# Two sequences per scan, VectorE in GpSimd's place, blocks of 512 tokens, and weight tiles in pairs: one kernel of attention and two MoE layers

## The chip, the core and the metric

One of the eight cores of a Trainium2 chip runs the kernel: TensorE (matmuls, PE in the profile, with PEld for its weight loads), VectorE (DVE), ScalarE (ACT), GpSimd (POOL) and SyncE (SP, which issues the DMA transfers here). The metric is the device time of one execution in microseconds. Three runs of the kernel before took 1298.25, 1298.7 and 1300.54 us, a median of 1298.7.

## What is computed

The reference, cut to what matters. Four sequences of 768 tokens, 8 heads of width 48, go through a recurrence with a complex decay; its output, 3072 tokens of 384 values, goes through two dense layers with different activations (`moe` and `moe2`; nothing is routed).

```python
# q, k, v, a_re, a_im: (4, 8, 768, 48)
mag = np.sqrt(a_re * a_re + a_im * a_im)
scale = np.minimum(mag, 0.999) / (mag + 1e-06)
a_re_n, a_im_n = (a_re * scale, a_im * scale)
for t in range(S):
    ar, ai = (a_re_n[:, :, t, :, None], a_im_n[:, :, t, :, None])
    new_re = ar * S_re - ai * S_im
    new_im = ar * S_im + ai * S_re
    kv = np.einsum('bhd,bhe->bhde', k[:, :, t], v[:, :, t])
    S_re, S_im = (new_re + kv, new_im)
    y[:, :, t] = np.einsum('bhd,bhde->bhe', q[:, :, t], S_re)
x = y.transpose(0, 2, 1, 3).reshape(3072, 384)
h = x @ w_in                                   # w_in (384, 2048)
x = (h * (1.0 / (1.0 + np.exp(-1.702 * h)))) @ w_out   # w_out (2048, 384)
h = x @ w2_in
out = (h - np.tanh(h)) @ w2_out
```

The weights come as float64 (random numbers of numpy) and are handed to the device as pairs of 32-bit words.

## The kernel before

**Attention.** A sequence is cut into 6 chunks of 128 tokens (`C`), so there are 24 sequence chunks (`NU`), worked on in the order of chunk number first and sequence second. A chunk passes four generators. `s1` (L342) scales the decay and runs the first level of a prefix product: 16 runs (`NS`) of 8 tokens (`L`) lie on the partitions with the heads, and the loop over `j` (L371) multiplies complex numbers along a run. `s2` (L381) carries the products across the 16 runs in four doubling steps, each of which shifts data between partitions by a DMA (L391). `s3` (L403) multiplies both together (L410 to L414), divides k by the product and multiplies q with it (L438, L441). `s4` (L445) transposes both on TensorE (L465), makes scores (L479), masks them (L481), forms y from the state (L488) and from the chunk (L492), and updates the state of the sequence (L502 to L513). `transposed` (L518) then splits the chunk's 384 values per token into a rounded part `xh` and a rest `xl` for matmuls.

GpSimd shares the elementwise work: `PT` is its two-input operation (L349 to L368, L410, L438, L513, and in the MoE layers L203 and L248), `TT` and `STT` are those of VectorE, `ACT` those of ScalarE. The first three chunks (`BORROW`) use buffers of the weights.

**The MoE layers.** A block is 384 tokens (`TB`, three chunks, `BU`), so there are 8 blocks for each of the two layers. `moe` (L527) runs, for each block and each of the 16 tiles `f` of 128 hidden values, `h_tile` (9 matmuls into bank `h`: three chunks of the contraction, each as rounded times rounded, rounded times rest, rest times rounded, L138 to L140), a gate (`gate1` or `gate2_small`, which also splits its result into `gh` and `gl`), and `out1` or `out2` (9 matmuls into the banks `o`, and in the second layer `y`), three steps later (`LAG`). Each matmul streams 384 columns. Two sets of `xh` and `xl` exist (L143). The first layer's output goes to DRAM (`store1`) and comes back for the second (`load_o`).

**Weights.** `wsplit` (L97) turns one tile of 128 x 384 float64 weights into a rounded part and a rest: two operations on ScalarE, four on VectorE (L111 to L114), a rounding copy on ScalarE (L116), a product, a difference and a sum on GpSimd (L117, L119, L121; the very first tile's difference on VectorE, as are those of the second layer). There are 32 tiles in each layer.

**Order.** Every generator is given a start and an end (`add`, L601), by tables and rates (`SLOT`, `DC`, `BL`, L606 to L672); the steps of all are sorted by due time and emitted (L675), and a scheduler then orders each engine's queue. An engine runs its queue in that order.

PSUM has eight banks: `h` 2, `at` 2, `o` 3, `y` 1 (L91). A second path (from L682) recomputes everything if a range check failed; it is not taken with these inputs.

Of the kernel before, what the change touches and what calls it, by code (L numbers as in the profile page):

```python
# [41 lines left out]
def attention_moe_moe(ctx, tc, q, k, v, a_re, a_im, w1_in, w1_out, w2_in, w2_out, out):  # L42
# [11 lines left out]
    TB = 3 * C  # L54
# [30 lines left out]

    h4 = cp.tile([P, NBLK * NF], F32, name="h4")

    GL = 5
    BORROW, WA = 3, 8
    SQ = 1  # L90
    BANKS = {"h": 2, "at": 2, "o": 3, "y": 1}  # L91

    def psum(pool, tag, bufs):
        return pool.tile([P, 512], F32, tag=tag, name=tag, bufs=bufs)


    def wsplit(pools, wpool, tag, bufs, src, name, rawpool=None, sub=None):  # L97
        cm = pools["cm"]
        rp, rtag, rbufs = rawpool or (cm, "raw", 2)
        raw = rp.tile([P, 2 * DM], I32, tag=rtag, name=rtag, bufs=rbufs)  # L100
        dma(out=raw.rearrange("p (c x) -> p c x", c=src.shape[1]), in_=src)
        yield
        w3 = raw.rearrange("p (n w) -> p n w", w=2)
        lo32, hi32 = w3[:, :, 0], w3[:, :, 1]
        w = wpool.tile([P, 2, DM], F32R, tag=tag, name=tag, bufs=bufs)
        v_ = cm.tile([P, DM], F32, tag="cv", name="cv", bufs=3)
        vi, l_ = v_.bitcast(I32), lo32.bitcast(F32)
        ACT(out=v_, in_=hi32.bitcast(F32), func=AF.Abs, scale=65536.0)
# [18 lines left out]
    def w_in_src(src, f):  # L127
# [680 lines left out]
```

## Time and profile before

| | us |
|---|---|
| median of three runs | 1298.7 |
| the profiled execution | 1300.61 |
| its span, first to last instruction | 1298.9 |
| first matmul of the first MoE layer, block 0 | 175.2 |
| block 1 | 298.4 |
| block 7, the last of the first layer | 814.8 |
| first block of the second layer | 877.0 |
| its second block | 934.8 |
| last matmul | 1286.2 |

The starts of blocks are those of each block's first h matmul (288 matmuls make a block). Durations of VectorE and ScalarE reach from start to written result, and neighbours overlap a little, so that the distance of two starts is what an operation takes in a full queue. GpSimd's spans are rough. TensorE's ends are modelled; distances of starts are exact.

### The profile page before, as it was taken

How to read it: one execution, taken by the hardware profiler on the slowest of the kernel's cores; microseconds unless marked ns; L12 is line 12 of the kernel's file. 1: busy time of each engine (PE TensorE's matmuls, PEld its weight loads, DVE VectorE, ACT ScalarE, POOL GpSimd, SP SyncE). 2: the span in 40 equal slices, each digit the busy share in tenths (PEclk: the TensorE clock that was granted, in tenths of full speed). 3: DMA queues.
4: the chain of work that ended last, by engine and by line, in shares of the span. 5: the costliest groups of instructions: out<-in, count | busy, mean ns of one | idle time of the engine just before them, and what ended most of it. 6: DMA issues, size and time to landing. Idle time of an engine off the chain costs nothing.

```text
span 1298.9 us, 19212 instructions
## 1 busy us (share of the span) xinstructions
PE 1086.9 (84%) x6496; PEld 1057.8 (81%) x6496; DVE 891.3 (69%) x2089; ACT 735.5 (57%) x1553; POOL 582.1 (45%) x482
## 2 busy tenths in 40 slices
PE   0004678789979999999999999978999999999996
PEld 0004668778979988999988998878999999999996
DVE  6998999989988778878687729898333333333332
ACT  4323454555645464454464536667767777777673
POOL 5676767664533333333333205667434434434331
PEclk9999578788889899989998998999999999999998
DMA  5112322333213112232231104441001001000000
GB/s 170 58 49 84 94 73 75 102 88 85 61 45 81 51 51 67 54 83 54 57 81 41 46 21 144 139 122 37 28 10 37 19 19 38 13 25 25 1 19 24
DMA packets 114052, 77.01 MB, mean 59 GB/s; under 512 B 69904, under 2 KB 109840, under 8 KB 113936
## 3 DMA queue, kind: packets, MB, share of 16 engines
q1 hardware_dynamic: 113936, 75.61, 20.8%
q8 instruction: 55, 0.90, 0.3%
q14 instruction: 61, 0.50, 0.1%
HBM read 53.48 MB, written 9.44 MB: 48 GB/s over the span
## 4 chain that ended last, share of the span: by engine, by line
PE 42%; DVE 30%; ACT 7%; DMA 6%; POOL 6%; issue 6%; SPq 0%; DVEq 0%; POOLq 0%; ACTq 0%
PE o L139 5%; PE o L140 5%; PE o L138 5%; PE h L138 4%; PE h L140 4%; PE h L139 4%; DVE a L376 3%; DMA shifted<-x 3%; PE at L138 3%; PE at L140 3%; PE at L139 3%; DVE cv L113 2%; DVE gl L167 2%; DVE pq L373 2%; DVE cv L111 2%
## 5 line engine op out<-in xcount | busy, mean ns | idle before, releaser
L197 DVE SCALAR_TENSOR_TENSOR q<-q,u 128x384 f32<-128x384 f32 x128 | 75.6, 591 | 237.5 <-ACT q L196 237.2
L203 POOL TENSOR_TENSOR gl<-q,gh 128x384 fp32r<-128x384 f32 x128 | 132.3, 1036 | 234.2 <-ACT gh L202 198.8
L138 PE MATMUL h<-xh,wb 128*128 128x384 f32 x384 | 136.8, 356 | 15.9 <-DVE gl L167 15.9
L140 PE MATMUL h<-xh,wb 128*128 128x384 f32 x384 | 135.0, 352 | 0.0
L139 PE MATMUL h<-xl,wb 128*128 128x384 f32 x384 | 133.6, 348 | 0.0
L202 ACT ACTIVATE gh<-q 128x384 fp32r<-128x384 f32 x128 | 67.1, 524 | 78.2 <-DVE q L198 70.8
L139 PE MATMUL o<-gl,wb 128*128 128x384 f32 x288 | 103.1, 360 | 1.7 <-DVE gl L167 1.7
L140 PE MATMUL o<-gh,wb 128*128 128x384 f32 x288 | 102.0, 356 | 0.0
L167 DVE TENSOR_TENSOR gl<-h,gh 128x384 fp32r<-128x384 f32 x128 | 70.4, 550 | 40.1 <-ACT h L165 37.8
L438 POOL TENSOR_TENSOR kh<-a,sz 128x768 f32<-128x768 f32 x24 | 49.9, 2080 | 106.4 <-PE at L465 58.3
L138 PE MATMUL o<-gh,wb 128*128 128x384 f32 x288 | 93.2, 357 | 3.5 <-ACT gh L164 3.4
L164 ACT ACTIVATE gh<-h 128x384 fp32r<-128x384 f32 x128 | 62.2, 486 | 56.7 <-PE o L140 42.0
L138 PEld LDWEIGHTS h<-xh,wb 128*128 128x128 f32 x384 | 75.1, 196 | 21.8 <-DVE gl L167 21.1
L454 PE MATMUL at<-ident,scratch 128*96 128x128 f32 x1 | 0.4, 421 | 100.5 <-DVE scratch L429 100.5
L196 ACT ACTIVATE q<-u,qb 128x384 f32<-128x384 f32 x128 | 78.8, 616 | 9.6 <-POOL gl L203 0.3
L454 PEld LDWEIGHTS at<-ident,scratch 128*96 128x96 f32 x1 | 0.2, 156 | 100.5 <-POOL qz L410 100.5
L410 POOL TENSOR_TENSOR qz<-a,x 128x768 f32<-128x768 f32 x21 | 50.2, 2392 | 66.8 <-DVE x L399 66.8
L368 POOL TENSOR_TENSOR a<-a,sc 128x768 f32<-128x768 f32 x24 | 49.4, 2058 | 58.2 <-DVE sc L367 58.2
L140 PEld LDWEIGHTS h<-xh,wb 128*128 128x128 f32 x384 | 75.4, 196 | 0.0
L139 PEld LDWEIGHTS h<-xl,wb 128*128 128x128 f32 x384 | 75.0, 195 | 0.1
L492 PEld LDWEIGHTS y<-vt,at 128*128 128x128 f32 x368 | 53.7, 223 | 24.0 <-DVE at L481 23.9
L492 PE MATMUL y<-vt,at 128*128 128x48 f32 x368 | 56.2, 306 | 19.5 <-DVE at L481 19.3
(263 smaller groups left out, 3735.6 us busy)
## 6 DMA issues: line engine op xcount, KB each, us to landing
raw<-in_moe_w_in_dram SPq DMA_DIRECT2D x32, 384.0 KB
ks<-kh SPq DMA_DIRECT2D x160, 48.0 KB
raw<-in_moe_w_out_dram SPq DMA_DIRECT2D x18, 384.0 KB
wb<-in_moe_w_out_dram SPq DMA_DIRECT2D x14, 384.0 KB
a<-in_a_re_dram SPq DMA_DIRECT2D x24, 192.0 KB
a<-in_a_im_dram SPq DMA_DIRECT2D x24, 192.0 KB
kt<-in_k_dram SPq DMA_DIRECT2D x24, 192.0 KB
qt<-in_q_dram SPq DMA_DIRECT2D x24, 192.0 KB
```

The costliest lines, as they stand in the source:

```text
L138: MM(dst, a[0], b[0], start=first, stop=False)
L139: MM(dst, a[0], b[1], start=False, stop=False)
L140: MM(dst, a[1], b[0], start=False, stop=last)
L164: ACT(out=gh, in_=hp, func=AF.Gelu_apprx_sigmoid)
L167: TT(out=gl, in0=hp, in1=gh.bitcast(F32), op=SUB)
L196: ACT(out=q, in_=u, func=AF.Square, bias=qb[:, 2:3])
L197: STT(q, q, SMALL_B, u, op0=ADD, op1=MUL)
L202: ACT(out=gh, in_=q, func=AF.Copy)
L203: PT(out=gl, in0=q, in1=gh.bitcast(F32), op=SUB)
L410: PT(out=qz, in0=z, in1=over_l(x[:, 1]), op=MUL)
L438: PT(out=kh.rearrange("p j c d -> p c j d"), in0=z, in1=both(kw), op=MUL)
L492: MM(y[h], ats[h], vt[:, h], start=first and h == 0, stop=h == H - 1)
```

## The change

**Scan.** Two sequences' chunks (`NP`) go through `s1`, `s2` and `s3` at once: 12 pairs instead of 24 chunks, each instruction twice as wide, except those that make `pz`, `qz`, `kh` and `qh`, which stay single. `s4` stays per chunk. Buffers of `kh`, `qh`, `kT`, `qT`, `ks` and `vt` are single for all chunks, and the first chunks borrow no weight buffers.

**GpSimd.** Everything that it did beside VectorE goes to VectorE. The range check of the decay becomes a fused add-and-minimum (L355 of the new kernel) and an accumulated sum on ScalarE.

**Blocks.** A block is 512 tokens, the same 128 of each of the four sequences: 6 blocks for each layer, matmuls of 512 columns (`out2` keeps 384). x of a block is made in one go (`block_x`) after its four chunks, in one set of `xh` and `xl` in the first layer; the second layer alternates between two pools. `LAG` is 2. `gh`, `gl` and the outputs on their way to DRAM share five buffers. A block of the second layer takes all four output banks.

**Weights.** Two tiles are converted together (16 pairs in each layer). In the first layer, the difference and the sum are made by TensorE: the value times the identity, minus the rounded part times the identity, plus the low part, in PSUM, and a copy by ScalarE.

The table of due times is rewritten for this. The core of the diff:

```diff
-    TB = 3 * C
+    NP = 2
+    NT = NU // NP
+    TB = B * C
...
+    nident = cp.tile([P, P], F32R, name="nident")
+    ACT(out=nident, in_=ident, func=AF.Copy, scale=-1.0)
...
+    def wsplit(wp, vp, raw, name, by_pe=None):
...
+        TT(out=l_, in0=l_, in1=t_, op=MUL)
+        yield
+        if by_pe:
+            for i in range(2):
+                wp_ = psum(ps, by_pe)[:, :DM]
+                MM(wp_, ident, v_[:, i], start=True, stop=False)
+                MM(wp_, nident, w[:, i, 0], start=False, stop=False)
+                MM(wp_, ident, l_[:, i], start=False, stop=True)
+                ACT(out=w[:, i, 1], in_=wp_, func=AF.Copy)
+            yield
+        else:
+            TT(out=t_, in0=v_, in1=w[:, :, 0].bitcast(F32), op=SUB)
+            yield
+            TT(out=w[:, :, 1], in0=t_, in1=l_, op=ADD)
...
-        return [pools["cm"].tile([P, KC, TB], F32R, tag=n_, name=n_, bufs=2) for n_ in ("xh", "xl")]
+    def split_tiles(pool, bufs=1):
+        return [pool.tile([P, KC, TB], F32R, tag=n_, name=n_, bufs=bufs) for n_ in ("xh", "xl")]
...
+    def gpair(pool):
+        return [gtile(pool, n_, bufs=5, tag="g") for n_ in ("gh", "gl")]
...
-        PT(out=gl, in0=q, in1=gh.bitcast(F32), op=SUB)
+        TT(out=gl, in0=q, in1=gh.bitcast(F32), op=SUB)
...
+    O1, O2 = ["o"] * KC, ["o"] * KC + ["y"] * (BU - KC)
...
+            ot = gtile(pools["cm"], "ot", F32, 5, "g")
...
+        nc.vector.tensor_tensor_reduce(out=flat(m2), in0=flat(m2), in1=flat(ys), scale=1.0, scalar=3e38, op0=ADD, op1=ALU.min, accum_out=amin[:, u:u + 1])
...
-        PT(out=qz, in0=z, in1=over_l(x[:, 1]), op=MUL)
-        TT(out=pz, in0=z, in1=over_l(x[:, 0]), op=MUL)
+        for n in range(NP):
+            z = a[:, :, n]
+            pz, qz = t3("pz"), t3("qz")
+            TT(out=qz, in0=z, in1=over_l(x[:, 1, n]), op=MUL)
+            TT(out=pz, in0=z, in1=over_l(x[:, 0, n]), op=MUL)
...
-        PT(out=kh.rearrange("p j c d -> p c j d"), in0=z, in1=both(kw), op=MUL)
+            kh, qh = [sp.tile([P, L, 2, D], F32, tag=n_, name=n_, bufs=1) for n_ in ("kh", "qh")]
+            TT(out=kh.rearrange("p j c d -> p c j d"), in0=z, in1=both(kw[:, n]), op=MUL)
...
-    def transposed(xp, xs, x, col):
+    def block_x(pools, x, xs):
+
         for c in range(KC):
-            nc.tensor.transpose(xp[:, c * P:(c + 1) * P], xs[:, c * P:(c + 1) * P], ident)
+            xp = psum(pools["ps"], "at")
+            for t in range(BU):
+                nc.tensor.transpose(xp[:, t * C:(t + 1) * C], xs[t][:, c * P:(c + 1) * P], ident)
+            ACT(out=x[0][:, c], in_=xp, func=AF.Copy)
+            TT(out=x[1][:, c], in0=xp, in1=x[0][:, c].bitcast(F32), op=SUB)
...
-    LAG = 3
+    LAG = 2
...
+            edge = s_ < len(todo) and n == 1 and f == 0 and m
+            if edge:
+                gate(s_ - 1)
...
+                    XT[m] = split_tiles(R["cm"])
+                    block_x(R, XT[m], [XS[m, b // NP][:, b % NP] for b in range(B)])
+                if edge:
+                    output(s_ - 1)
...
-    SLOT, SLOT0, T0, B0, DB = 29.44, 26.5, 63.96, 22.34, 10
+    SLOT, T2, T3, T4, BL = 50, 112, 148, 190, 64
```

What the new table does to the queues shows in three places. First VectorE in `s3`, in the middle of the first layer; before (L411, L413, L414 of one chunk, its qz made by GpSimd, between a gate's gl, another chunk's scan and qh):

```order
L411 TENSOR_TENSOR pz_4468<-a3_3608,x_4324 128x768
L167 TENSOR_TENSOR gl_4383<-h_4336,gh_4380 128x384
L394 TENSOR_TENSOR pq2_4402<-x_4366,shifted0_109 128x96
L395 TENSOR_TENSOR pq2_4403<-x_4366,shifted0_109 128x96
L413 TENSOR_TENSOR a3_3608<-pz_4468,qz_4469 128x384
L441 TENSOR_TENSOR qh_4276<-a3_3279,qt_3953 128x2x8x48
L414 TENSOR_TENSOR a3_3608<-pz_4468,qz_4469 128x384
```

Now, from the first qz of a pair on:

```order
L419 TENSOR_TENSOR qz_3608<-a_2802,x_3573 128x768
L420 TENSOR_TENSOR pz_3607<-a_2802,x_3573 128x768
L182 TENSOR_TENSOR gl_3664<-h_3582,gh_3663 128x512
L384 TENSOR_TENSOR a_2802<-pz_3607,qz_3608 128x384
L385 TENSOR_TENSOR a_2802<-pz_3607,qz_3608 128x384
```

The product qz, GpSimd's before, stands in VectorE's own queue, and the gate's gl waits behind both.

Second TensorE where one block of the first layer ends and the next begins; before (o is the output of the old block, h of the new one, and the transposes of xs are those of a later chunk):

```order
L138 MATMUL o_3692<-gh_4519,wb_1566 128x384
L139 MATMUL o_3692<-gl_4522,wb_1566 128x384
L140 MATMUL o_3692<-gh_4519,wb_1566 128x384
L520 MATMUL at_4327<-ident_61,xs_4313 128x128 x3
L138 MATMUL o_3693<-gh_4519,wb_1566 128x384
L139 MATMUL o_3693<-gl_4522,wb_1566 128x384
L140 MATMUL o_3693<-gh_4519,wb_1566 128x384
L138 MATMUL o_3694<-gh_4519,wb_1566 128x384
L139 MATMUL o_3694<-gl_4522,wb_1566 128x384
L140 MATMUL o_3694<-gh_4519,wb_1566 128x384
L138 MATMUL h_4509<-xh_3613,wa_194 128x384
L138 MATMUL h_4596<-xh_3613,wa_243 128x384
```

Now, at the same place (the old block's last output, then a chunk's y and state, the next chunk's transposes, and the new block's x):

```order
L156 MATMUL o_3488<-gh_4348,w_1271 128x512
L498 MATMUL y_4198<-vt_3999,at_4148 128x48 x4
L507 MATMUL at_4258<-vt_3999,ks_4134 96x48 x3
L498 MATMUL y_4198<-vt_3999,at_4184 128x48 x4
L507 MATMUL at_4258<-vt_3999,ks_4134 96x48 x5
L464 MATMUL at_4307<-ident_61,gr_4196 96x128
L473 MATMUL at_4318<-ident_61,kh_4267 96x128 x4
L473 MATMUL at_4342<-ident_61,qh_4268 96x128 x4
L522 MATMUL at_4355<-ident_61,xs_3512 128x128 x2
L522 MATMUL at_4355<-ident_61,xs_4009 128x128 x2
L522 MATMUL at_4362<-ident_61,xs_3512 128x128 x2
L522 MATMUL at_4362<-ident_61,xs_4009 128x128 x2
```

The h matmuls of the new block, which went straight behind the last o, now come behind the transposes of the x that they read.

Third TensorE inside block 0; before (one h tile, then outputs):

```order
L138 MATMUL h_1630<-xh_987,wa_294 128x384
L139 MATMUL h_1630<-xl_988,wa_294 128x384
L140 MATMUL h_1630<-xh_987,wa_294 128x384
L139 MATMUL o_1716<-gl_1605,wa_219 128x384
L140 MATMUL o_1716<-gh_1602,wa_219 128x384
```

Now (raw is a pair of weight tiles in conversion, at the bank of its sum):

```order
L156 MATMUL h_1211<-xh_989,w_407 128x512
L154 MATMUL o_1161<-gh_1156,w_288 128x512
L155 MATMUL o_1161<-gl_1157,w_288 128x512
L156 MATMUL o_1161<-gh_1156,w_288 128x512
L154 MATMUL o_1162<-gh_1156,w_288 128x512
L155 MATMUL o_1162<-gl_1157,w_288 128x512
L156 MATMUL o_1162<-gh_1156,w_288 128x512
L154 MATMUL o_1163<-gh_1156,w_288 128x512
L132 MATMUL at_1130<-raw_1032,ident_61 128x384
L133 MATMUL at_1130<-w_1123,nident_73 128x384
L134 MATMUL at_1130<-raw_1032,ident_61 128x384
```

The three matmuls of a weight sum stand between those of block 0, seven pairs in all there.

## Rows read from the trace of the kernel before

**Rows 1.** Page, parts 1 and 4: busy time per engine; the last chain.

```profile
PE 1086.9 (84%) x6496; PEld 1057.8 (81%) x6496; DVE 891.3 (69%) x2089; ACT 735.5 (57%) x1553; POOL 582.1 (45%) x482
...
PE 42%; DVE 30%; ACT 7%; DMA 6%; POOL 6%; issue 6%; SPq 0%; DVEq 0%; POOLq 0%; ACTq 0%
```

**Rows 2.** Stretches: length, busy us PE, PEld, DVE, ACT, POOL; PEclk, DMA.

```profile
0.00:175.20 175.20, 43.78 (x237) 40.59 (x238) 152.95 (x387) 63.72 (x130) 117.64 (x93) 0.87 0.33 93
175.20:298.40 123.20, 99.41 (x574) 93.53 (x573) 115.72 (x247) 67.50 (x128) 82.14 (x68) 0.86 0.29 81
298.40:814.80 516.40, 486.65 (x3093) 471.35 (x3094) 400.57 (x1072) 274.72 (x509) 178.74 (x127) 0.94 0.24 64
814.80:877.00 62.20, 52.72 (x290) 49.72 (x290) 57.99 (x101) 39.96 (x89) 36.94 (x37) 1.00 0.45 134
877.00:934.80 57.80, 52.59 (x290) 51.47 (x289) 36.37 (x58) 41.70 (x103) 34.48 (x33) 0.97 0.10 28
934.80:1286.20 351.40, 351.40 (x2018) 351.12 (x2017) 127.66 (x228) 246.62 (x592) 132.17 (x128) 1.00 0.06 21
```

**Rows 3.** TensorE in order of time: start us, us, line, operation.

```profile
214.46 0.69 PE L138 MATMUL h<-xh,wb 128*128 128x384 f32 x1 [2.73 <-DVE gl L167]
214.94 0.52 PE L139 MATMUL h<-xl,wb 128*128 128x384 f32 x1
215.26 0.52 PE L140 MATMUL h<-xh,wb 128*128 128x384 f32 x1
...
605.37 1.95 PE L479 MATMUL at<-qT,kT 96*128 96x128 f32 x16
...
612.09 2.74 PE L492 MATMUL y<-vt,at 128*128 128x48 f32 x16 [2.12 <-DVE at L481]
...
1001.96 0.34 PE L139 MATMUL o<-w,gh 128*128 128x384 f32 x1
1002.13 0.34 PE L140 MATMUL o<-w,gl 128*128 128x384 f32 x1
```

**Rows 4.** VectorE in order of time, 98 to 105 us.

```profile
98.46 1.82 DVE L427 TENSOR_SCALAR scratch<-scratch 128x48 int32<-128x48 int32 x1
...
100.78 0.95 DVE L411 TENSOR_TENSOR pz<-a,scratch 128x768 f32<-128x768 f32 x1
101.65 0.25 DVE L376 TENSOR_TENSOR a<-pq,pq 128x96 f32<-128x96 f32 x1
101.82 0.24 DVE L430 TENSOR_TENSOR phase<-a,scratch 128x96 f32<-128x96 f32 x1
...
103.67 0.54 DVE L413 TENSOR_TENSOR a<-pz,qz 128x384 f32<-128x384 f32 x1
104.14 0.54 DVE L414 TENSOR_TENSOR a<-pz,qz 128x384 f32<-128x384 f32 x1
```

**Rows 5.** GpSimd in order of time, 94 to 130 us.

```profile
98.27 1.96 POOL L410 TENSOR_TENSOR qz<-a,scratch 128x768 f32<-128x768 f32 x1 [0.86 <-DVE scratch L399]
105.63 8.79 POOL L438 TENSOR_TENSOR kh<-a,sz 128x768 f32<-128x768 f32 x2 [5.40 <-ACT sz L416]
```

**Rows 6.** Single lines of VectorE: count, duration ns min/median/max.

```profile
L411 DVE TENSOR_TENSOR pz<-a,x x21: 943/959/2569, 128.2 to 739.1; 128x768 f32<-128x768 f32 x21
...
L111 DVE TENSOR_SCALAR cv<-cv x64: 345/353/2004, 15.0 to 890.8; 128x384 f32<-128x384 f32 x64
...
L481 DVE TENSOR_TENSOR at<-at,mask x44: 675/682/692, 123.1 to 800.3; 128x512 f32<-128x512 f32 x44
```

**Rows 7.** A GpSimd group: count, busy us, mean ns, idle, releasers.

```profile
L410 POOL TENSOR_TENSOR qz<-a,x 128x768 f32<-128x768 f32 x21 | 50.2, 2392 | 66.8 <-DVE x L399 66.8
```

**Rows 8.** VectorE's first operation on data, TensorE's first instruction.

```profile
7.22 0.56 DVE L349 TENSOR_TENSOR sq<-sq 128x384 f32<-128x384 f32 x1 [4.85 <-ACT sq L347]
...
100.54 0.42 PE L454 MATMUL at<-ident,scratch 128*96 128x128 f32 x1 [100.54 <-DVE scratch L429]
```

**Rows 9.** Timeline of the end, SP's issues of the last outputs.

```profile
1286.74 3.10 SPq L240 DMA_DIRECT2D out_dram<-gl  x3
```

More of the change, by code (lines that the diff above doesn't have):

```diff
@@ L514, in s4 @@
+            TT(out=state[b], in0=state[b] if not first else kv, in1=gain, op=MUL)
         carried[b] += 1
[L515 removed]
         yield
[L518 removed]
+    def block_x(pools, x, xs):
         for c in range(KC):
[L520 to L523 removed]
@@ L549, in moe @@
+                hps[s_] = h_tile(R, w_in(n, f), XT[m] if n == 1 else O[m])
+            if not edge:
+                low(s_ - LAG)
+                gate(s_ - 1)
                 if s_ == len(todo):
                     check_h()
[L551 to L570 removed]
+                output(s_ - LAG)
@@ L575, in fetch @@
     def fetch(m):
-        O[m] = load_o(R, slice(m * TB, (m + 1) * TB))
+        O[m] = load_o(R, [(part, to) for to, part in block(m)], R["cm"] if m % 2 else R["sp2"])
         yield
@@ L639, in attention_moe_moe @@
-    for w_ in range(2 * NF):
-        f, o = divmod(w_, 2)
-        src = (w_in_src(w1_in, f), w_out_src(w1_out, f))[o]
-        t = 8 + w_ * CE if w_ < 8 else C0 + w_ * DC
-        raws = (R["w"], "wb", 2 * NF - WA) if w_ % 2 and w_ < 28 else None
-        add(wsplit(R, R["w"], *wslot(w_), src, (1, "io"[o], f), raws, PT if w_ else TT), 6, t - 3.4, t + 3.4)
-    end = at(NU + 1)
-    starts = [at(4 + m * BU) + (DB if m else B0) for m in range(NBLK)]
-    t = starts[-1] = max(starts[-1], end + DB)
@@ new lines, in attention_moe_moe, with words @@
+    for u in range(NT):
+        add(once(load_a, u), 1, *(2 * [-5 + u if u < 2 else span("s3", u - 2)[1]]))
+        add(once(load_qk, u), 1, *(2 * [1 if not u else span("s3", u - 1)[1]]))
+        add(s1(u), NS1, *span("s1", u))
+        add(s2(u), NS2, *span("s2", u))
+        add(s3(u), NS3, *span("s3", u))
+    for i in range(NU):
+        add(once(load_v, i), 1, *(2 * [span("s4", i)[0] - 6]))
+        add(s4(i), NS4 - (i // B == NG - 1), *span("s4", i))
+    raws = {}
+    def words(n, f, rp):
+        raws[n, f] = wload(R, *((w1_in, w1_out) if n == 1 else (w2_in, w2_out)), f, rp)
+        yield
@@ new lines, in conv @@
+    def conv(n, f, wp, vp, by_pe=None):
+        yield from wsplit(wp, vp, raws.pop((n, f)), (n, f), by_pe)
+    wb = (R["w"], "wb", WB)
+    C1 = [20, 26, 32, 38, 46, 54, 62, 70] + [80 + 5.3 * n for n in range(NF - 8)]
+    for f, t in enumerate(C1):
+        add(words(1, f, wb if f < NF - 3 else (sa, "t6", 2)), 1, *(2 * [t - 14]))
+        add(conv(1, f, wb, wb if f < NF - 2 else (sa, "t3", 2), "o" if f < 7 else "at"), 5, t - 4, t + 4)
+    starts = [82] + [T[2 * m + 1] + 1.45 * SLOT for m in range(1, NBLK)]
@@ L652, in attention_moe_moe @@
+    starts += [starts[-1] + BL * (m + 1) for m in range(NBLK + 1)]
     feed = moe()
```

548 lines of the change are left out of this document (248 added, 300 removed).

## Prediction

> **What bounds the kernel now.** I read the shares of the whole span first, then the stretches between block starts, then single rows of TensorE, VectorE and GpSimd. TensorE is busy 84% of the span and has 42% of the chain that ended last, but VectorE has 30% of that chain and GpSimd 6% [rows 1], so the bound changes on the way, and the stretches show where [rows 2]. In the first 175.2 us VectorE is busy 153 and GpSimd 118 of them, TensorE 44; the first MoE matmul starts at 175.2, and TensorE's first instruction of all at 100.5, released by VectorE [rows 8]. Block 0 (384 tokens) then takes 123.2 us, VectorE busy 115.7 of them. From 298.4 to 814.8 six blocks take 516.4, or 86.1 each, with TensorE busy 94% of it. Block 7, the last of the first MoE, and the first of the second take 62.2 and 57.8, with VectorE busy 93% and 63%. The last seven blocks take 351.4, 50.2 each, and TensorE is busy in all of it.
>
> So three rates matter. A block is 288 matmuls, so one costs 50.2/288 = 0.174 us; two neighbours do start 0.17 apart, and 0.32 apart at the lower of the two clock levels, 1.2 GHz against 2.4 [rows 3]. In the middle a block takes 86.1 - 50.2 = 36 us longer for the three sequence chunks of attention put into it: 12 us per chunk, with its own matmuls, its waits and the share of time at the lower level (granted clock 0.94) in it. A wait of that sort is the 2.12 us before the y matmuls of 612.09, released by VectorE's masked product [rows 3].
>
> **GpSimd and VectorE.** Alone, VectorE starts a 768-wide two-input operation 0.87 us before the next, a 384-wide one 0.47, a 96-wide one 0.17 [rows 4]. Beside GpSimd a 48-wide operation took 1.82 us, just while GpSimd's qz ran from 98.27 for 1.96; and two kh of GpSimd took 8.79 us while VectorE's queue was full [rows 4, 5]. Lines of one form run from 943 to 2569 ns and from 345 to 2004 [rows 6]. With lone prices for all 2089 of its instructions VectorE would need 636 us; it was busy 891 [rows 1]. A factor of 1.4 is waiting for the other engine, and most of it lies ahead of 300 us.
>
> **What the change does to VectorE.** It gets all of GpSimd's work (a mean of 2.39 us for qz [rows 7]) and fewer, wider instructions. Prices, from starts: 0.87 for 768, 0.47 for 384, 0.17 for 96 [rows 4]; for 192 between the last two I take 0.27 on the straight line; for 512 0.60 (0.68 of duration [rows 6] less the 0.08 by which a duration exceeds a start-to-start); tensor_scalar 384 is 0.345 - 0.08 = 0.27, so 768 is 0.47. One pair of chunks costs 18 x 0.87 + 23 x 0.27 + 22 x 0.17 + 4 x 0.47 in s1 to s3, and 4 x 0.60 + 4 x 0.47 in its two s4: 32 us with the small ones, 12 pairs 388 us. A pair of weight tiles costs 3 x 0.47 + 2 x 0.87 = 3.15, and 4.9 in the second MoE, where VectorE also makes the sums. The one form that the trace lacks is the fused add-and-minimum of 768: between one and two operations, 0.87 to 1.74, 12 times, 10 us over the run at most; I take 0.9, as it reads two inputs as the others do.
>
> *Start.* Ahead of the first xl, VectorE's order holds 69 operations of 768 (60 us), 36 tensor_scalar of 768 (17), 68 of 192 (18), 66 of 96 (11), 14 of 384 (7), 8 of 512 (5): 120 us with the rest, 12 of the 16 weight pairs among them. Before, the first operation that needs data began at 7.22 [rows 8]; now it waits for twice the loads and a Square of twice the width, and a second round through ScalarE follows: 12 us idle. Four chunks then go through TensorE's transposes, scores and y on an engine that idled, one after another through single kh, qh, kT and qT; before, three such took from 100.5 to beyond 170. I add 14 for waits there. First h matmul at 146, for 512 tokens instead of 384.
>
> **What it does to TensorE.** Columns are the same, 6 blocks of 512 for 8 of 384. No 512-wide matmul is in the trace. Its bounds: 0.213 us if it has nothing beyond its columns (0.32 at the lower level is 0.833 ns a column, half of it at the upper), 0.232 if the 0.174 scale with width. I take what one matmul has beyond its columns as fixed, 0.174 - 0.160 = 0.014, hence 0.228. A block of the first MoE is 288 of them, 65.5 us (61.4 to 66.9); one of the second 144, and 192 of 384, 66.2 (64.2 to 66.9). Over 12 blocks the bounds are 37 less and 13 more.
>
> The Trainium skill (TensorE: Matmul & The Clock Gate, Back-to-back issue gap) gives N/2.4 + 2.5 ns, 216 ns here and 162 at 384 columns; the sum by it would be 30 us lower. At 384 the rows have 174, so I stay with the rows.
>
> *Sums of weights.* Per tile two fp32 matmuls of 384 columns and one rounded one. Eight fp32 products of 128 columns fill 1.95 us [rows 3], about 0.22 each, so 384 columns take 0.67, and a pair 2 x (2 x 0.67 + 0.17) = 3.0 us. Nine pairs come ahead of the first h matmul, on an engine that idles there; seven are inside block 0: 21 us on the path. Bounds: 7 (every pass as the rounded one) and 43 (all at the lower level). What they take off VectorE is 1.74 us a pair, 28 in all.
>
> **The sum** (span). Start 146. Block 0: 65.5, four chunks at 12, the sums 21: 135; VectorE's order has 110 us in the same stretch, so TensorE is late by little. Blocks 1 to 4: 65.5 + 48 = 113.5 each, 454; VectorE has 74 to 76 us of work in each. I leave the 12 us per chunk as it is: waits for VectorE shrink, but x now has one buffer, so that each block's transposes and split come after the last h of the block ahead. Block 5: 70, for VectorE has 61 us of conversions and gl in it, without GpSimd in its way. Second MoE: 6 x 66.2 plus under 1 us at each edge, since a block now takes all four output banks and the copies hide behind one h: 402. Tail 13, from the last matmul's 1286.2 to the end at 1298.9 before [rows 2]. Together 1220. Around the span lie 1.7 us (the profiled execution took 1300.6), and that execution is 1.9 above the median of 1298.7, so 1220 stands for the median too.
>
> Where the 79 us come from: block 0 ends at 281 with 512 tokens done; before, that state was reached at about 298 + 86/3 = 327, so 46. From there 512 tokens took 114.8, so four blocks gain 5. The last 512 tokens of the first MoE took 86.1/3 + 62.2 = 91, now 70: 21. The second MoE took 57.8 + 351.4 = 409, now 402: 7.
>
> **The rivals.**
> *More gain.* With GpSimd silent the waits behind the masked product go, and the lower level that follows each: 12 us per chunk become 10 (20 chunks, 40 us), and wide matmuls come out near 0.22 (20 us): 1160. For it: TensorE's gaps of 298 to 815 mostly end with VectorE. Against it: the y of a chunk still hangs on one product in VectorE's queue, now behind operations of 0.87 us.
>
> *One x buffer decides.* At each of five edges nothing of the next block may run on TensorE until transposes, a ScalarE copy, a VectorE subtraction and then the first gate are through, some 5 us, and a pause of 2 to 3 us was followed by the lower level before (0.32 spacing behind the gap that ends at 214.46 [rows 3]). At 10 us an edge the sum is 1270. A block's outputs also share five buffers with gh and gl now, and leave SP in 12 transfers; three of the tail take 3.1 us [rows 9], so 12 us at most, in which the second and third gate of the next block want those buffers. I cost that at nothing, since two h and one out of 2 us each run first; without that cover it is 5 us an edge, inside this case. Against it: the order puts the next chunk's transposes and scores into these holes.
>
> The Trainium skill (Trainium Kernel Development and Optimization, Best Practices) asks for double buffers so that loads and work overlap; it speaks against the one x buffer of the first MoE, and by it this rival would be the likelier. No row of the kernel before shows a block edge with a single buffer.
>
> *Slower.* VectorE's slow operations were not GpSimd's doing (but that of transfers or ScalarE on the same memory). Then the change only moves 582 us of GpSimd's busy time onto the busiest early engine. At a factor of 1.4 the start is 48 us longer, block 0 19, blocks 1 to 4 4 each, block 5 and the first block of the second MoE 15 and 20: 1338. It overtakes the kernel before from a factor of about 1.27. Against it speak the normal rows between 100.3 and 105 with GpSimd still [rows 4, 5].
>
> *It doesn't act.* VectorE's waits are covered by something else ahead of 300 us (weight transfers): the 46 and the 21 us fall away, and 2 us at each of five edges go to the one x buffer: 1297.
>
> **Chances.** Forecast 1220 (1190 to 1250) 0.50; more gain 0.20; one x buffer 0.17; slower 0.10; no action 0.03. The range for 8 in 10 is 1150 to 1285: it leaves out the slower case and the ends of the others. Faster by over 0.2% 0.87, within 0.2% 0.03, slower 0.10; 0.2% is about what a measurement of this kernel can tell.
>
> **What would show it.** Right: a VectorE line of one form has one duration, within 5%, from start to end; the first h matmul lies at 135 to 160; block starts 108 to 118 us apart; 0.22 to 0.23 between wide matmuls. Wrong: the start above 170, or more than 125 us between starts with VectorE over 90% busy (slower), or TensorE idle over 5 us ahead of each block's first h (one x buffer), or over 4 us per pair of sums.

## The result: faster by 1.4%, where 6% was forecast

The changed kernel took 1279.4 us (median of four runs, 1278.4 to 1284.4), the kernel before 1298.5 (1297.4 to 1300.5): a ratio of 0.986, 95% interval 0.983 to 0.989. It is faster by 19 us. The forecast was 1220, so the direction was right and the gain four times too large; the time lies just inside the range, whose upper end was 1285.

The profiled execution has a span of 1277.4 us. First its page: busy time by engine, and the chain that ended last, which answer to [rows 1].

```profile
PE 1132.6 (89%) x5792; PEld 961.4 (75%) x5792; DVE 819.8 (64%) x1607; ACT 665.5 (52%) x1130; POOL 1.1 (0%) x8
...
PE 56%; DVE 18%; DMA 10%; ACT 6%; SPq 6%; issue 3%; DVEq 0%; ACTq 0%
```

GpSimd is silent, and VectorE is busy for 820 us where it was for 891, with all of GpSimd's work on top. In the chain that ended last, transfers have 10% where they had 6, and SyncE's issuing of transfers (SPq) 6% where it had none. Then the stretches, cut at the first h matmul, the starts of block 1 and block 5, the first h matmul of the second layer and the last matmul. Columns as in [rows 2]: length, busy us of PE, PEld, DVE, ACT, POOL, the granted clock, DMA share and GB/s.

```profile
0.00:167.80 167.80, 91.38 (x358) 68.26 (x358) 125.14 (x290) 72.69 (x104) 1.09 (x8) 0.71 0.43 126
167.80:351.80 184.00, 155.25 (x737) 128.32 (x737) 117.11 (x254) 77.45 (x119) 0.00 (x0) 0.80 0.19 50
351.80:791.30 439.50, 413.79 (x2391) 345.67 (x2389) 299.22 (x648) 215.21 (x331) 0.00 (x0) 0.98 0.24 63
791.30:860.10 68.80, 68.34 (x293) 54.33 (x294) 57.09 (x83) 40.96 (x62) 0.00 (x0) 1.00 0.41 132
860.10:1267.40 407.30, 403.69 (x2019) 364.81 (x2017) 220.38 (x333) 258.67 (x515) 0.00 (x0) 1.00 0.07 21
```

| | forecast | measured | difference |
|---|---|---|---|
| first h matmul | 146 | 167.8 | +22 |
| block 0 | 135 | 184.0 | +49 |
| blocks 1 to 4 | 454 | 439.5 | -14 |
| block 5 | 70 | 68.8 | -1 |
| second layer | 402 | 407.3 | +5 |
| tail | 13 | 10.2 | -3 |
| span | 1220 | 1277.4 | +57 |

Everything that is missing is missing before 351.8 us. The state "512 tokens through the first layer" came at about 327 before, was forecast for 281, and comes at 351.8. From there to the end the kernel before needed 972 us and the changed one 926: 46 less, where 33 were forecast.

In block 0, VectorE is busy for only 117 of 184 us, against 116 of 123 (for 384 tokens) before. Its longest waits there, from 168 to 352 us, by line, releaser, us in total, times and longest:

```profile
DVE p L399 <- DMA before<-x: 17.7, 8, 4.5
DVE gl L182 <- PE o L155: 8.5, 2, 4.7
DVE cv L119 <- ACT cv L116: 7.9, 3, 6.4
DVE gl L182 <- ACT w L135: 6.6, 1, 6.6
...
DVE kh L449 <- DMA ks<-kh: 3.9, 2, 2.1
```

The first is the scan's wait for shifted data, a quarter of the 67 us that VectorE idles there; the second and fourth are a gate's gl that waits for TensorE's outputs and for ScalarE's copy of a weight sum. Over the whole run the wait for shifted data comes to much more than at the same step (L394) of the kernel before; first this kernel's row, then that one's:

```profile
DVE p L399 <- DMA before<-x: 85.5, 39, 5.5
```

```profile
DVE pq L394 <- DMA shifted<-x: 25.9, 20, 5.4
```

And this is TensorE from the end of block 0's matmuls on, in order of time (start us, us, operation, and in brackets the idle time before it and what ended it):

```profile
266.66 0.40 PE L156 MATMUL o<-gh,w 128*128 128x512 f32 x1
...
288.06 0.42 PE L464 MATMUL at<-ident,gr 128*96 128x128 f32 x1 [2.49 <-DVE gr L438]
293.09 1.06 PE L473 MATMUL at<-ident,kh 128*96 128x128 f32 x4 [4.61 <-DVE kh L449]
...
337.13 0.42 PE L464 MATMUL at<-ident,gr 128*96 128x128 f32 x1 [5.59 <-DVE gr L438]
343.03 1.06 PE L473 MATMUL at<-ident,kh 128*96 128x128 f32 x4 [5.48 <-DVE kh L449]
...
348.17 0.60 PE L522 MATMUL at<-ident,xs 128*128 128x128 f32 x4
```

All 288 matmuls of block 0 are done at 267. For the next 81 us TensorE has no MoE work at all: x of block 1 needs chunk 7, and chunks 5 to 8 go through it one after another, waiting for VectorE in turn. Their own matmuls keep it busy 51 of 75 us, at the lower clock level (granted 0.50):

```profile
271.00:346.00 75.00, 50.59 (x241) 46.94 (x242) 52.90 (x130) 18.77 (x30) 0.00 (x0) 0.50 0.24 62
```

The chain that ended last shows which engine the stretch waited for. From 168 to 242 us it lies on TensorE alone. Of the 85 us from 267 to 352 it has 38 on VectorE, 14 on transfers, 13 on TensorE and 11 on SyncE, which issues a chunk's ks transfers 0.6 us apart. The lower clock level can account for some 7 us of the 85 at most, by this estimate: half of the 13, since 16 score matmuls take 3.78 us there and took 1.95 at the upper level [rows 3].

### The profile page after: what moved, and what is told of

Same layout as the page of the kernel before. It is cut to its first block, busy times and chain, and to the rows that moved or that the text cites. A ratio compares the mean times of both kernels' runs of the same rounds, so it can differ in the third digit from the quotient of the medians.

```text
span 1277.4 us, 15921 instructions
## 1 busy us (share of the span) xinstructions
PE 1132.6 (89%) x5792; PEld 961.4 (75%) x5792; DVE 819.8 (64%) x1607; ACT 665.5 (52%) x1130; POOL 1.1 (0%) x8
## 4 chain that ended last, share of the span: by engine, by line
PE 56%; DVE 18%; DMA 10%; ACT 6%; SPq 6%; issue 3%; DVEq 0%; ACTq 0%
PE o L155 6%; PE o L156 6%; PE o L154 6%; PE h L154 5%; PE h L155 5%; PE h L156 5%; DMA before<-x 5%; PE at L156 3%; PE at L155 3%; PE at L154 3%; SPq L480 3%; DMA raw<-in_moe_w_out_dram 2%; PE at L485 2%; PE y L498 1%; PE y L155 1%
## 5 line engine op out<-in xcount | busy, mean ns | idle before, releaser
L154 PE MATMUL h<-xh,w 128*128 128x512 f32 x432 | 175.9, 412 | 14.7 <-ACT xh L523 6.0
L155 PE MATMUL h<-xl,w 128*128 128x512 f32 x432 | 174.4, 404 | 0.0
L156 PE MATMUL h<-xh,w 128*128 128x512 f32 x432 | 172.2, 399 | 0.0
L213 DVE SCALAR_TENSOR_TENSOR q<-q,u 128x512 f32<-128x512 f32 x96 | 66.4, 691 | 108.9 <-ACT q L212 108.9
L155 PE MATMUL o<-gl,w 128*128 128x512 f32 x288 | 115.4, 401 | 0.8 <-DVE gl L182 0.7
L156 PE MATMUL o<-gh,w 128*128 128x512 f32 x288 | 115.5, 401 | 0.0
L154 PEld LDWEIGHTS h<-xh,w 128*128 128x128 f32 x432 | 81.7, 190 | 36.3 <-DVE gl L182 9.2
L154 PE MATMUL o<-gh,w 128*128 128x512 f32 x288 | 104.5, 402 | 1.0 <-ACT gh L180 0.9
L154 PE MATMUL o<-w,gh 128*128 128x384 f32 x288 | 97.3, 338 | 0.0
L155 PE MATMUL o<-w,gh 128*128 128x384 f32 x288 | 96.9, 337 | 0.0
L156 PEld LDWEIGHTS h<-xh,w 128*128 128x128 f32 x432 | 81.8, 189 | 18.2 <-issue 0.3
L155 PEld LDWEIGHTS h<-xl,w 128*128 128x128 f32 x432 | 82.0, 190 | 15.0 <-DVE xl L524 0.6
L156 PE MATMUL o<-w,gl 128*128 128x384 f32 x288 | 90.8, 337 | 0.0
L212 ACT ACTIVATE q<-u,qb 128x512 f32<-128x512 f32 x96 | 69.3, 721 | 2.4
```

The lines of the kernel that those rows point to most:

```text
L154: MM(dst, a[0], b[0], start=first, stop=False)
L155: MM(dst, a[0], b[1], start=False, stop=False)
L156: MM(dst, a[1], b[0], start=False, stop=last)
L212: ACT(out=q, in_=u, func=AF.Square, bias=qb[:, 2:3])
L213: STT(q, q, SMALL_B, u, op0=ADD, op1=MUL)
```

## The experiments

The theory from these rows had three parts: (A) silencing GpSimd works as forecast; (B) the new scan is a chain (shifts, single buffers, order) that leaves VectorE idle; (C) TensorE's sums cost more than their 21 us. Times are medians of four runs (ten for e12), with the kernel before run beside them on the same chip (medians of 1295.4 to 1298.4, so that 3 us between two kernels may be the chips').

### GpSimd alone

The kernel before, with nothing changed but the engine:

```diff
-    PT = nc.gpsimd.tensor_tensor
+    PT = nc.vector.tensor_tensor
```

> The kernel before with GpSimd's elementwise work (its 482 operations) on VectorE and nothing else changed. At lone start-to-start prices VectorE's work is 884 us instead of 636. Theory 1 (VectorE's slow operations were GpSimd's doing): every line of VectorE has one duration, busy time near 930 (overlapping durations), first h matmul near 167, block 0 near 108 us instead of 123, the last block of the first layer and the first of the second near 52 each: 1262. Rival (the slow operations have another cause): VectorE busy above 1100 and the time above 1320. Second rival (GpSimd's removal is worth nothing here, since the scan's chain of transfers sets the early stretch): 1290 to 1300.

1214.2 us, ratio 0.937 (0.934 to 0.941). One line brings 84 us, more than the 79 that the forecast gave to the whole change, and 48 more than was expected of this run. VectorE's single lines (count, ns min/median/max), the 96-wide product of the scan before and here, and the tensor_scalar of [rows 6] here:

```profile
L374 DVE TENSOR_TENSOR pq<-a x147: 240/251/1911, 56.4 to 717.0; 128x96 f32<-128x96 f32 x147
```

```profile
L374 DVE TENSOR_TENSOR pq<-a x147: 245/249/259, 43.6 to 654.7; 128x96 f32<-128x96 f32 x147
...
L111 DVE TENSOR_SCALAR cv<-cv x64: 343/350/363, 15.3 to 828.9; 128x384 f32<-128x384 f32 x64
```

What ranged up to 1911 ns has one duration. Of VectorE's operations that take over 10% longer than the shortest of the same line and form, the excess adds up to some 205 us in the kernel before and to under 1 us here. Its stretches up to block 1:

```profile
0.00:80.00 80.00, 0.00 (x0) 0.00 (x0) 69.33 (x253) 30.64 (x55) 2.34 (x14) 1.00 0.39 111
80.00:160.90 80.90, 50.71 (x269) 47.96 (x270) 75.87 (x226) 37.29 (x81) 0.00 (x0) 0.71 0.32 90
160.90:253.80 92.90, 79.01 (x462) 73.55 (x461) 90.01 (x265) 58.06 (x111) 0.00 (x0) 0.90 0.33 94
```

VectorE is busy 145 of the first 161 us and 90 of the next 93: with GpSimd's work on it, it has hardly a gap. Here 512 tokens are through at 253.8 + 89.0/3 = 283.5 us (block 2 starts at 342.8; as in the kernel before, these starts count 288 matmuls a block, and the next block's first h matmul comes earlier, at 287.7 instead of 298.4 in that kernel). That is close to the 281 forecast for the changed kernel. So (A) holds, and the rest of the change loses 65 us. The run does not part two gains: VectorE's operations are no longer stretched, and GpSimd's slow operations leave the chain that ended last, of which they had 6% [rows 1], some 75 us. The reverse, two products given back to GpSimd in the changed kernel:

```diff
-            TT(out=qz, in0=z, in1=over_l(x[:, 1, n]), op=MUL)
+            PT(out=qz, in0=z, in1=over_l(x[:, 1, n]), op=MUL)
...
-            TT(out=kh.rearrange("p j c d -> p c j d"), in0=z, in1=both(kw[:, n]), op=MUL)
+            PT(out=kh.rearrange("p j c d -> p c j d"), in0=z, in1=both(kw[:, n]), op=MUL)
```

> The changed kernel with qz and kh, 48 operations of 768, back on GpSimd. VectorE's work falls by 42 us. Theory (GpSimd's elementwise work beside VectorE stretches VectorE's operations): operations of VectorE beside them take up to 2.5 times as long, GpSimd's own take 2.1 to 2.4 us, and the scan's chain gets longer by 1.2 to 1.5 us for each of them on it: 1290 to 1310. Rival (VectorE's load counts, not its neighbour): block 0 gets shorter, 1260 to 1275.

1297.8 us (1.001, 0.999 to 1.003), as the theory had it: 48 operations on GpSimd take back the whole gain of 18. That excess of VectorE's operations is some 25 us here, and GpSimd takes 2.1 to 2.3 us for an operation that takes VectorE 0.95; how the 18 us divide between the two is not shown. One VectorE line beside them, and GpSimd's two groups (count, busy us, mean ns, idle before):

```profile
L420 DVE TENSOR_TENSOR pz<-a,x x24: 937/952/2562, 65.3 to 736.2; 128x768 f32<-128x768 f32 x24
```

```profile
L419 POOL TENSOR_TENSOR qz<-a,x 128x768 f32<-128x768 f32 x24 | 55.0, 2293 | 301.9 <-DVE x L385 119.8 <-DVE raw L127 67.4 <-DMA raw<-in_moe_w_out_dram 63.3
L449 POOL TENSOR_TENSOR kh<-a,sz 128x768 f32<-128x768 f32 x24 | 50.0, 2084 | 356.1 <-DVE sz L444 156.2 <-PE at L473 57.3 <-DMA ks<-kh 39.6
```

In the changed kernel pz takes 949 to 964 ns in all 24 cases.

The longest pz beside GpSimd takes 1.61 us more than the median, less than one operation of GpSimd. The Trainium skill (SBUF — State Buffer, SBUF: two separate sides) has the two engines share a port pair that one of them holds for a whole instruction while the other blocks, for VectorE's operations with two inputs in SBUF, as this one, among others; the size here fits that, and no row shows the pair itself.

### The sums of weights

All sums on VectorE, and then only those ahead of the first h matmul on TensorE:

```diff
-        add(conv(1, f, wb, wb if f < NF - 2 else (sa, "t3", 2), "o" if f < 7 else "at"), 5, t - 4, t + 4)
+        add(conv(1, f, wb, wb if f < NF - 2 else (sa, "t3", 2), None), 5, t - 4, t + 4)
```

> The changed kernel with the differences and sums of the first layer's weights on VectorE instead of TensorE and ScalarE: 1.74 us more per pair there, 28 in all, and 17 us less for TensorE inside block 0. Prediction's term (21 us of sums on the path of block 0): block 0 17 us shorter, the start 5 to 16 us later, 1265 to 1280. Theory B: block 0 is not shorter, since its matmuls end at 267 and the pairs' chain ends at 351, and VectorE's extra work makes that chain later: 1285 to 1300.

1257.9 us, 21.5 less than the changed kernel. The start is 23 us later (190.9), block 0 takes 143.9: 40 us less. That is faster than both cases expected.

```diff
+        add(conv(1, f, wb, wb if f < NF - 2 else (sa, "t3", 2), ("o" if f < 7 else "at") if f < 9 else None), 5, t - 4, t + 4)
```

> The changed kernel with TensorE's sums for the nine pairs ahead of the first h matmul, and VectorE's for the seven inside block 0. In the changed kernel VectorE stands idle for most of 172 to 210: gl waits for TensorE's sums and ScalarE's copies of them, and pair 3's scan stands behind gl in VectorE's queue (its first operation at 210; with all sums on VectorE at 172). Theory (the ring of sum, copy and gl inside block 0 delays the scan): the first h matmul stays near 168, pair 3's scan starts before 190, block 0 takes 145 to 155 instead of 184: 1240 to 1250. Rival (the later start, 191, is what shortened block 0 with all sums on VectorE, since work was only shifted ahead of it): block 1 starts at 335 or later, 1258 to 1265.

1260.6 us: the rival's time was right. Both kernels reach block 1 at 335 to 337, so it makes no difference whether TensorE or VectorE does the early sums here; the seven inside block 0 are what costs, 17 to 19 us. The rival's reason (the later start shortened block 0) is not needed: here the start is at 169.8 and block 0 still takes 17 us less. A sum's price shows in the changed kernel:

```profile
175.80 0.84 PE L132 MATMUL at<-raw,ident 128*128 128x384 f32 x2
176.17 0.65 PE L133 MATMUL at<-w,nident 128*128 128x384 f32 x1
176.66 0.84 PE L134 MATMUL at<-raw,ident 128*128 128x384 f32 x2
177.02 1.18 PE L154 MATMUL o<-gh,w 128*128 128x512 f32 x3
178.04 0.84 PE L132 MATMUL at<-raw,ident 128*128 128x384 f32 x2
```

From one sum to the next are 2.24 us with three wide matmuls (0.70) between, so a pair costs 3.1 us and seven pairs 22. Part (C) falls: the term of 21 was right. The early sums do pay in a kernel in which VectorE is full. In the kernel before without GpSimd, the first 16 of 64 tiles:

```diff
+        if by_pe:
+            wp_ = psum(ps, by_pe, BANKS[by_pe])[:, :DM]
+            MM(wp_, ident, v_, start=True, stop=False)
+            MM(wp_, nident, w[:, 0], start=False, stop=False)
+            MM(wp_, ident, l_, start=False, stop=True)
+            yield
+            ACT(out=w[:, 1], in_=wp_, func=AF.Copy)
...
-        add(wsplit(R, R["w"], *wslot(w_), src, (1, "io"[o], f), raws, PT if w_ else TT), 6, t - 3.4, t + 3.4)
+        add(wsplit(R, R["w"], *wslot(w_), src, (1, "io"[o], f), raws, PT if w_ else TT, "o" if w_ < 16 else None), 6, t - 3.4, t + 3.4)
```

> The kernel before without GpSimd, with the difference and sum of its first 16 weight tiles (of 64) on TensorE and ScalarE, as the change does it for all. VectorE was busy 90% and more until 254 us there, and saves 16 x 0.94 = 15 us. Theory (sums on TensorE pay where TensorE idles and VectorE is full): first h matmul at 146 to 152 instead of 161, 1200 to 1206. Rival (the transposes of the first chunks then wait behind sums in TensorE's queue, and VectorE behind those): 1212 to 1222.

1198.7 us, ratio 0.926 (0.924 to 0.928), first h matmul at 153.6, block 1 at 240.4. It is the fastest kernel of this study, 81 us below the changed one.

### Buffers and order

Two buffers of kh, and x of block 1 with an earlier due time:

```diff
-            kh, qh = [sp.tile([P, L, 2, D], F32, tag=n_, name=n_, bufs=1) for n_ in ("kh", "qh")]
+            kh, qh = [sp.tile([P, L, 2, D], F32, tag=n_, name=n_, bufs=nb_) for n_, nb_ in (("kh", 2), ("qh", 1))]
```

> The changed kernel with two buffers of kh instead of one (qh, kT, qT, ks and vt stay single). In the changed kernel VectorE waits 10.8 us in all for the transfers that read kh, 6.9 of them ahead of the first h matmul. Theory B (chain of pairs, its single buffers in it): the first h matmul near 158 instead of 168, block 0 5 us shorter, 1262 to 1268. Theory A or the half clock alone: under 4 us of change, 1274 to 1280.

1267.2 us, first h matmul at 160.3: 12 us, half ahead of the first h matmul.

```diff
-    starts = [82] + [T[2 * m + 1] + 1.45 * SLOT for m in range(1, NBLK)]
+    starts = [82, T[3] + 60] + [T[2 * m + 1] + 1.45 * SLOT for m in range(2, NBLK)]
```

> The changed kernel with the x of block 1 put ahead of chunk 8's transposes in the due times. In the changed kernel chunk 7's y ends at 331, and TensorE then waits, mostly for VectorE's work on chunk 8, until 348 before it transposes x. Theory A (the order at that edge is what costs): block 1 starts at 333 to 338 instead of 352, and the end comes 12 to 16 us earlier, near 1265. Theory B (the chain of pairs through transfers and VectorE sets the pace): block 1 starts as early, but block 2 starts at about the same 463, and the time is 1275 to 1280.

1268.8 us, block 1 at 338.4 and block 2, too, 10 us earlier: 11 us. Each looked like a separate cost. Together, with all sums on VectorE, and then with the early ones on TensorE:

> The changed kernel with three edits at once: two kh buffers, x of block 1 ahead of chunk 8, all sums on VectorE. Alone they gave 12, 10 and 21 us. If they are separate costs: 1279 - 43 = 1236. If they are one wait seen from three sides (the scan's chain from pair to pair): 1250 to 1256, near the best single one.

> The changed kernel with TensorE's sums only ahead of the first h matmul, two kh buffers and the x of block 1 first. If the costs are separate: the first h matmul near 160, block 1 near 300, and 1220 to 1228, which is the forecast of the prediction and still slower than the kernel before without GpSimd (1214). If they are one wait: 1235 to 1245.

1251.3 and 1256.2 us. The parts (21, 12 and 11; 19, 12 and 11) don't add up to 44 and 42; 28 and 23 remain, the second outside both cases expected. In the first of the two, TensorE showed a reason why x was still late, one transpose left ahead of it:

```profile
318.45 0.42 PE L464 MATMUL at<-ident,gr 128*96 128x128 f32 x1 [19.35 <-DVE gr L438]
318.66 1.06 PE L522 MATMUL at<-ident,xs 128*128 128x128 f32 x4
```

So x went ahead of that one, too (due at `T[3] + 56.5`):

> The kernel with three edits (two kh buffers, x of block 1 earlier, all sums on VectorE), with x of block 1 moved 3.5 units of due time further ahead, so that in TensorE's queue it also passes the transpose of chunk 8's gain. With three edits x's sources were complete at 299, and TensorE stood 19.4 us at that one transpose, for VectorE's gr at 318, before it took x. Theory (the order at the first edge was still wrong; one transpose was left in front): block 1 starts at 300 to 304 and 12 to 19 us come off, 1232 to 1239. Rival (VectorE and the scan's chain set the pace anyway): block 1 starts early and block 2 at the same 441, 1246 to 1252.

1262.2 us, slower, and outside both cases. Block 1 starts at 306.9 instead of 320.4, and then takes 143.9 us instead of 120.7; block 2 starts at 450.8 instead of 441.1. The chunks that block 2 needs are not what is late: chunk 11's y is through at 428 (432 with the three edits), and block 1's matmuls were done by 411. TensorE then waits for the next chunk, whose transposes stand ahead of the x of block 2 in its queue:

```profile
426.20 1.91 PE L498 MATMUL y<-vt,at 128*128 128x48 f32 x8
441.31 0.42 PE L464 MATMUL at<-ident,gr 128*96 128x128 f32 x1 [13.21 <-DVE gr L438]
447.20 1.06 PE L473 MATMUL at<-ident,kh 128*96 128x128 f32 x4 [5.47 <-DVE kh L449]
```

So the fault of the first edge stands at the second as well, and moving one edge alone moved the wait there. A kernel with both edges in the other order was not run; whether the idle 19 us are lost time stays open.

### One sequence per scan

```diff
-    NP = 2
+    NP = 1
...
-        a = A[u] = sa.tile([P, 2, NP, L, D], F32, tag="a", name="a", bufs=2)
+        a = A[u] = sa.tile([P, 2, NP, L, D], F32, tag="a", name="a", bufs=4)
...
-            sh = before[k_]
+            sh = before[u % 2 * len(LEVELS) + k_]
```

(and the other buffers of the scan alike; each chunk is due in its half of the pair's time.)

> The changed kernel with one sequence per scan (24 scans of one chunk, twice as many buffers of half the size, each chunk's scan in the half of its pair's due time); the sums stay on TensorE. VectorE's work rises by about 4 us per pair, 50 in all, 17 of them ahead of block 1. Theory (a pair's chain of transfers, 85 us of VectorE's waits for the shifted data, sets the pace, and more chains in flight hide it): waits for shifted data fall below 45 us, block 1 starts before 340, 1255 to 1270. Rival (pairs only save work): block 1 starts at 360 or later and the time is 1285 to 1310.

1269.3 us, 10 less than with pairs, although VectorE has some 50 us more to do; the wait for shifted data is 77 us over 47 times. The time fell into the theory's range, the waits did not fall below 45 us as it wanted. With the edits of e9, one kh buffer apart:

> The same early x and sums on VectorE, with one sequence per scan and one kh buffer. If scanning in pairs costs by itself (one sequence per scan was 10 us faster beside sums on TensorE): 5 to 12 us below the kernel with pairs of the same call, or the same with its two kh. If the 10 us were only room in VectorE's queue while it waited for sums: VectorE's 50 us of added work come through in part, 5 to 15 us above it.

1260.8 us against 1262.2 with pairs: no difference beyond the runs' spread, with a kh buffer fewer and 53 us more work on VectorE. So scanning in pairs saves no time in either comparison, and costs 10 us beside sums on TensorE; what it costs in the second one is not separated from the kh buffer. The instructions that it saves are saved on an engine that waits.

### The table of due times

Only the due times of pairs 2, 3 and 4, and with them all later ones:

```diff
-    SLOT, T2, T3, T4, BL = 50, 112, 148, 190, 64
+    SLOT, T2, T3, T4, BL = 50, 90, 128, 168, 64
```

> The changed kernel with the due times of pair 2's, pair 3's and pair 4's scans at 90, 128 and 168 instead of 112, 148 and 190, everything behind them 22 earlier, and nothing else. In the changed kernel chunk 4's transposes come at 240, 102 us behind chunk 3's, since pair 2's third step stands in VectorE's queue behind block 0's gates and conversions, which wait for TensorE's sums. Theory (the table's gap is the cause): chunk 4's transposes at 205 to 225, block 1 and block 2 15 to 30 us earlier, 1250 to 1265. Rival (pairs and blocks themselves are too coarse, so that work put ahead of the gates delays block 0 by as much): the first h matmul 10 us later, block 2 where it was, 1272 to 1285.

1259.3 us, 20 less, by numbers alone: chunk 4's transposes at 205.5 instead of 239.9, block 1 at 333.6, block 2 at 442.8.

> The same table with all sums on VectorE, whose own time was 1258. Theory (gap): block 1 before 320 instead of 335, 1235 to 1248. Rival (coarse pairs and blocks): 1255 to 1265.

1245.2 us, the best of the changed kernel's family. Block 1 at 333.9 is hardly earlier than without the new table (334.8); block 2 is, at 436.7 (443.6). So the time fell into the theory's range without its sign, block 1 before 320.

> Pairs 2, 3 and 4 due at 78, 114 and 152, sums on VectorE. Theory (gap): a few us less than with 90, 128 and 168, 1228 to 1245. Rival: the first h matmul later by what block 1 gains, 1255 to 1270.

1262.0 us (78, 114, 152): worse than 90, 128, 168 by 17. The first h matmul is not later (191.7), so the rival's time came true without its reason; block 1 starts at 340.8.

> The kernel with three edits (1251) with pairs 2, 3 and 4 due at 90, 128 and 168. Theory (gap): block 1 before 305 instead of 320 and block 2 before 425 instead of 441, 1230 to 1240. Rival: 1248 to 1256.

1256.5 us, no better than the three edits with the old table. The gap in the table costs 13 to 20 us in two kernels and nothing in the third.

### What the runs have in common

| kernel | first h | block 1 | block 2 | time |
|---|---|---|---|---|
| changed | 167.8 | 351.8 | 462.8 | 1279.4 |
| e2, x earlier | 167.4 | 338.4 | 452.4 | 1268.8 |
| e3, two kh | 160.3 | 341.5 | 451.4 | 1267.2 |
| e4, sums on VectorE | 190.9 | 334.8 | 443.6 | 1257.9 |
| e6, all three | 180.1 | 320.4 | 441.1 | 1251.3 |
| e9, x earlier still | 180.1 | 306.9 | 450.8 | 1262.2 |
| e13, table | 167.7 | 333.6 | 442.8 | 1259.3 |
| e14, table, sums on VectorE | 191.6 | 333.9 | 436.7 | 1245.2 |

From block 2's start (1024 tokens through) to the end each takes 809 to 817 us. In the kernel before without GpSimd this state comes at 342.8 + 81.3 x 2/3 = 397, and 817 follow: the wide blocks, the pairs and the rest gain nothing later on. Nearly all that separates the kernels happens before block 2.

How far the MoE work has come when the scan has reached a chunk (matmuls of h and out counted in the traces, 288 being a block):

| when chunk 11's y ends | us | tokens through |
|---|---|---|
| before without GpSimd | 417.4 | 1121 |
| changed | 449.5 | 960 |
| e14 | 427.7 | 992 |

The changed kernel's scan is 32 us later at this point, and 161 tokens of matmuls behind (at 67 us per 512 tokens, 21 us); e14 is 10 us later and 129 tokens behind (17 us). That accounts for 53 of the 65, and 27 of the 31 that e14 still lacks. When chunk 7's y ends, the three have done 648, 512 and 512 tokens: a block of 512 cannot go on before its fourth chunk, while a block of 384 could. That the block size makes this backlog is argued from these counts; a kernel with 512-token blocks in the old scheme was not run. Why e14 is best among its neighbours is open, too; its wait for shifted data is the shortest of the family, 51.9 us against 89.1 in e4. And no run changed how SyncE issues the transfers, 6% of the chain that ended last.

## Why the prediction was right or wrong

**VectorE and GpSimd: right.** The forecast took lone prices for VectorE without GpSimd. Every line has one duration now, within 9% (pz 949 to 964 ns, the scan's products 347 to 361); the new fused operation, forecast at 0.9 us, takes 0.96 from start to result. e1 shows the mechanism by itself, e12 in reverse. The rival "slower" is out (its 4 us for each of blocks 1 to 4 does not follow from its own factor, either: 1.4 times 76 us is less than the 113.5 of the block).

**First h matmul, 146 against 167.8.** VectorE's 120 us of work were right (busy 125, with overlaps). Its waits were not: 12 us idle and 14 for the first chunks were put down, and it idles 43: 12 for ScalarE's squares at the head of a scan, as put down, 9 for shifted data, 7 for the transfers that read kh, 10 for TensorE, and smaller ones. A second kh buffer gives back 7 us (e3); the forecast had named it ("one after another through single kh, qh, kT and qT") under its 14 us, which were too few.

**Block 0, 135 against 184: the step that failed.** It added up TensorE's work, noted that "VectorE's order has 110 us in the same stretch, so TensorE is late by little", and so let the two engines run beside each other. They took turns. VectorE was busy 117 us and TensorE's matmuls were through at 267, after 99 us of which the sums took their forecast 21; then chunks 5 to 8 crossed TensorE one by one, and block 1 waited 85 us for them, of which the chain that ended last has 13 on TensorE. Two amounts of work, each smaller than the stretch, say nothing about the stretch as long as each waits for the other. The step that would have told was to follow one pair of chunks through both queues, from its first product to x, with the order of the changed kernel in hand.

**Where the 46 us came from.** The forecast credited the state "512 tokens through" with 46 us of gain from VectorE. The gain exists: e1 has nearly all of it (283.5). The change spent it again, and 25 more, on its own order.

**Wide matmuls.** 0.228 us were forecast between 0.213 and 0.232. Two neighbours start 0.23 apart (the median over all matmuls of h at the upper clock level is 0.232):

```profile
858.22 0.40 PE L155 MATMUL h<-xl,w 128*128 128x512 f32 x1
858.45 0.40 PE L156 MATMUL h<-xh,w 128*128 128x512 f32 x1
```

So the whole 0.174 scales with width, and nothing of it is fixed. The Trainium skill (TensorE: Matmul & The Clock Gate, Back-to-back issue gap), whose formula gives 216 ns at 512 columns, does not agree with the 232 of this trace; and by it, at both widths, the forecast's sum would have been some 45 us lower by estimate, not 30.

**Blocks 1 to 5, second layer, tail.** Within 15, 1, 5 and 3 us. A chunk costs (439.5 - 4 x 67)/16 = 10.7 us there instead of 12, part of what "more gain" wanted.

**The rivals.** "One x buffer decides" gave 1270 and came closest, for the wrong reason. It wanted 10 us at each of five edges; TensorE's waits for xh are small:

```profile
PE h L154 <- ACT xh L523: 6.0, 4, 4.2
```

6.0 us in all, 4.2 of them at block 1. That its time was near is luck. The Trainium skill (Trainium Kernel Development and Optimization, Best Practices) asks for double buffers so that transfers and work overlap; for kh, which transfers read, that gave 12 us (e3), and for x no run tried it. "More gain" is out, and so is "it doesn't act": it had other waits take the place of the slow operations, which is what happened, but it named the weight transfers, of which the largest group has 2% of the chain that ended last.

## What to carry to other kernels

Take an edit that removes contention apart from the edits that come with it: one line gave 84 us here, and the package around it cost 65 of them. If the saved instructions lie on an engine that waits in that stretch, count them as nothing. Where two engines hand work to and fro, a sum per engine is only a lower bound; price the stretch by following one item through all queues in the new order.

## What was not expected

The page's granted clock misleads where the trace has no record of it. From the first scores of chunk 0 into those of chunk 3, the same matmuls took 63.0 us in the changed kernel, at a granted clock of 0.50, and 66.3 in e4 (sums on VectorE), at 1.00, as if the lower level cost nothing:

```profile
89.80:152.80 63.00, 43.12 (x203) 39.40 (x204) 38.41 (x87) 17.45 (x27) 0.00 (x0) 0.50 0.35 97
```

```profile
113.80:180.10 66.30, 43.87 (x204) 39.36 (x204) 52.86 (x108) 22.87 (x34) 0.00 (x0) 1.00 0.36 102
```

But TensorE is busy for the same 43 to 44 us in both, and the 16 score matmuls of chunk 0 have the same duration, first in the changed kernel, then in e4:

```profile
89.77 3.79 PE L485 MATMUL at<-qT,kT 96*128 96x128 f32 x16 [0.68 <-ACT qT L474]
```

```profile
113.84 3.78 PE L485 MATMUL at<-qT,kT 96*128 96x128 f32 x16 [0.68 <-ACT qT L474]
```

At the upper level 16 such matmuls took 1.95 us [rows 3]. So both stretches ran at the lower level: e4's trace has its first record of the clock at 198.6 us, and the 1.00 ahead of it was not recorded. What the lower level costs in the start, no run here shows. A granted clock is to be read beside the duration of a known matmul.
